# A GEGLU by seven products on one core: the weight sums' first pair on VectorE, and two copies behind the second snapshot pair

## The chip, the cores and the metric

The kernel runs on one core of a Trainium2 chip. The time is that of the device in microseconds (us), from one launch on inputs that are already in its memory. The core has five engines that work side by side, each through a queue of its own: TensorE (PE in the profile, its weight loads PEld), VectorE (DVE), ScalarE (ACT), GpSimd (POOL) and SyncE (SP), which here issues the DMAs.

## What is computed

```python
B, S, Dm, Df = 1, 2048, 1024, 3584
def reference(x, w_gate, w_up, w_down):
    g = jnp.einsum("bsd,df->bsf", x, w_gate)
    u = jnp.einsum("bsd,df->bsf", x, w_up)
    h = _gelu(g) * u
    return jnp.einsum("bsf,fd->bsd", h, w_down)
```

`_gelu` is the tanh approximation. All inputs and the output are bfloat16.

## The kernel before

**Seven products in place of eight.** Each matrix product is cut into 2 x 2 blocks and formed with seven block products (the Strassen-Winograd scheme) instead of eight. The price is sums of blocks: of the activations (`t1` to `t4`, made once a pass), of the weights (`s1` to `s4`, made for every unit), and of the results, which are gathered in PSUM and in float32 copies. Blocks that enter a sum are kept as fp32r; blocks that enter a product alone are cast (`sa` from the weights, `tb` from the activations).

**Stages.** There are two passes of 1024 rows of x (`NPASS`). In each, the gate and up products come first, in 14 units, and then the down product (`down`). A unit is 256 of the 3584 hidden columns, in two blocks of 128, for both gate and up (`GU`), by 1024 rows in two blocks of 512. The result is gelu(gate) x up in `hT`. In the first pass the first 8 units (`R = 8`, called the early units here; units are counted from 0) are opened ahead of time: `opening()` forms their first results from raw bfloat16 weights, and keeps of each the product P1 in float32 copies (`p1s`). When a unit's turn comes, P1 is copied back into two PSUM banks, `seed(u + 1, ...)` (line 540), so that further products can be added to it.

**A unit** is written out in `unit` (line 221). TensorE runs five pairs of products, one for gate and one for up, of four 128x512 matmuls each: P2 (`s2`, `t2`) into the seeded banks `e`; P5 (`s1`, `t1`) into other banks; P3 (`s3`, `t3`) into `e`; then one with `s4` and `tb` into the banks of P5; and P4 (`sa`, `t4`) into `e`. In the profile P2, P5 and P3 are the groups `bank<-t,s`, the fourth is `bank<-tb,s` and P4 is `bank<-t,sa`. In between:

- ScalarE copies the two `e` banks after P2 (the snapshots u2, line 108) and the two banks of P5 (the snapshots p5, line 108). In the early units these land in a part of `xT`, so the profile shows them as `xT<-bank`.
- After u2, `behind_u2` seeds the next unit (two ScalarE copies, line 540).
- VectorE adds p5 to `e` (`sum`, and the same for up into a PSUM bank), later u2 to the other banks, and multiplies gelu by up (`hT`).
- `prepare` (called as `after_p5`) makes the next unit's weight sums: `s1`, `s2`, `s3`, `s4`, two each, all on GpSimd (line 94), and the two casts `sa` on ScalarE (line 103).

The products add into banks that others read: P3 waits for the u2 snapshots, the `tb` product for the p5 snapshots, P4 for VectorE's two sums.

**Down-weight sums.** From unit 2 of the first pass on, each unit also makes the sums of one block of the down weights (`keep_part`, line 278). They have three parts. For each, ScalarE copies a raw bfloat16 half into a free PSUM bank (`bank<-raw`, line 278) and VectorE subtracts (`m`, line 91). Part 0 stands ahead of the u2 snapshots, parts 1 and 2 behind the seeds, ahead of the p5 snapshots; part 2 also needs part 1's result. SyncE then stores the three sums to device memory (`store_made`, line 289, 768 KB) and, behind this in the same queue, loads the next unit's two raw halves (`fetch_wd`, line 270, 256 KB each), and behind that, in some units, gate and up weights (line 127).

**Order.** SyncE, VectorE, GpSimd and TensorE follow the order of the program text throughout (`ORDER`), and ScalarE does so in the gate and up stage. The kernel has no planner there: what is written first is issued first on its engine, and an instruction that waits holds up all behind it on that engine.

Of the kernel before, what the change touches and what calls it, by code (L numbers as in the profile page):

```python
# [10 lines left out]
def kernel(  # L11
# [48 lines left out]
    R = 8  # L60
# [22 lines left out]
    def slot(shape, dtype, name):  # L83
        return kpool.tile(shape, dtype, name=name, tag="k")
# [5 lines left out]
    def dve(out, a, b, op):  # L90
        nc.vector.tensor_tensor(out=out, in0=a, in1=b, op=op)  # L91
# [4 lines left out]
    def new(eng, a, b, op, name, shape=None, dtype=None):  # L96
        t = slot(shape or [P, N], dtype or f32r, name)
        eng(t, a, b, op)
        return t

    def cast(src, name, shape=None):
        t = slot(shape or [P, N], f32r, name)
        nc.scalar.copy(out=t, in_=src)  # L103
        return t

    def snap(ps, name, at=None):
        t = slot([P, N], f32, name) if at is None else at
        nc.scalar.copy(out=t, in_=ps)  # L108
        return t
# [25 lines left out]
    def block_of(w, n):  # L135
        return [w[:, i, :, n * P : (n + 1) * P] for i in range(2)]

    def block(ip, u, h):
        return u + R * h if ip == 0 and u < R else 2 * u + h
# [8 lines left out]
    def sums_t(xT):  # L148
        K = range(KH)
        lo, hi = [[xT[c][:, k] for k in K] for c in range(2)], [  # L150
            [xT[c][:, KH + k] for k in K] for c in range(2)
        ]
        return Sums(
            how={
                "t1": lambda q: [new(dve, lo[1][k], lo[0][k], SUB, "t1") for k in K],
                "t2": lambda q: [new(dve, hi[1][k], q["t1"][k], SUB, "t2") for k in K],
                "t3": lambda q, K=K: [new(dve, hi[1][k], lo[1][k], SUB, "t3") for k in K],
                "t4": lambda q: [new(dve, hi[0][k], q["t2"][k], SUB, "t4") for k in K],
                "tb": lambda q: [cast(hi[1][k], "tb") for k in K],
            }  # L160
        )

    def sums_s(w, eng):
        GU = range(2)
        sh = [P, KH, P]
        a11, a21 = [[w[h][i][:, :KH] for i in GU] for h in range(2)]
        a12, a22 = [[w[h][i][:, KH:] for i in GU] for h in range(2)]
        return Sums(
            how={
                "s1": lambda q, GU=GU: [new(eng, a21[i], a22[i], ADD, "s1", sh) for i in GU],  # L170
                "s2": lambda q: [new(eng, q["s1"][i], a11[i], SUB, "s2", sh) for i in GU],
                "s3": lambda q: [new(eng, a11[i], a21[i], SUB, "s3", sh) for i in GU],
                "s4": lambda q: [new(eng, a12[i], q["s2"][i], SUB, "s4", sh) for i in GU],
                "sa": lambda q: [cast(a22[i], "sa", sh) for i in GU],
            }
        )
# [6 lines left out]
        t.make("t1", "t2", "t3", "tb", "t4")  # L183
        return t

    def make_s(w, eng):
        s = sums_s(w, eng)
        s.make("s1", "s2", "s3", "sa", "s4")
        return s

    def gelu(src):
        g = slot([P, N], f32, "g")
        nc.scalar.activation(g, src, ACT.Gelu_apprx_tanh)  # L193
        return g

    def times(fb, c, g, u):
        dve(hT[:, fb // NJ, fb % NJ, c, :], g, u, MUL)

    def product(ps, lhs, rhs, start):
        for k in range(KH):  # L200
            matmul(ps, lhs[:, k, :], rhs[k], start and k == 0, k == KH - 1)
# [10 lines left out]
    def add(ps, other):  # L212
        g = new(dve, ps[0], other[0], ADD, "sum", dtype=f32)
        dve(ps[1], ps[1], other[1], ADD)
        return g, ps[1]
# [5 lines left out]
    def unit(fbs, banks, s, t, spare, behind_u2, after_p5, aside, keep, ahead_of_p4, behind_p4):  # L221
        GU = range(2)
        e, c, d = banks
        for i in GU:
            product(e[i], s["s2"][i], t["t2"], False)
        aside()
        keep(0, c[0])
        u2 = [snap(e[i], "u2", spare[i]) for i in GU]
        behind_u2()
        keep(1, c[0])  # L230
        keep(2, c[1])
        up = c[1]
        c = d
        for i in GU:
            product(c[i], s["s1"][i], t["t1"], True)
        p5 = [snap(c[i], "p5", spare[2 + i]) for i in GU]
        after_p5()
        for i in GU:
            product(e[i], s["s3"][i], t["t3"], False)
        g = new(dve, e[0], p5[0], ADD, "sum", dtype=f32)  # L240
        dve(up, e[1], p5[1], ADD)
        for i in GU:
            product(c[i], s["s4"][i], t["tb"], False)
        times(fbs[1], 1, gelu(g), up)
        g, up = add(c, u2)
        times(fbs[0], 1, gelu(g), up)
        ahead_of_p4()
        for i in GU:
            product(e[i], s["sa"][i], t["t4"], False)
        behind_p4()  # L250
        times(fbs[1], 0, gelu(e[0]), e[1])
# [108 lines left out]
    sa = {}  # L360
# [142 lines left out]
    first = [block_of(wa, u) for u in range(2)] + [block_of(mid, u) for u in range(4)]  # L503
    first += [block_of(end, u) for u in range(2)]

    def early(u):
        if u // 2 not in pairs_of:
            pairs_of[u // 2] = load_w((R + u) // 2, new_w())
        return [first[u], block_of(pairs_of[u // 2], u % 2)]
# [3 lines left out]
    s, t = sums_s(early(0), dve), sums_t(xT)  # L513
# [24 lines left out]
    def seed(u, e):  # L538
        for i in range(2):
            nc.scalar.copy(out=e[i], in_=p1s[u][i])  # L540
# [70 lines left out]
    def weights(ip, u):  # L611
        return early(u) if ip == 0 and u < R else loaded(u)

    for ip in range(NPASS):
        with tc.manual_schedule(engines={ENG.Activation}):
            if ip == 0:
                ws = {}
                nxt = opening()
            else:
                raw_of(0, F)()  # L620
                raw_of(1, C)()
            for u in range(NU):
                js = making(u) if ip == 0 else []

                def behind_u2():
                    if ip == 0 and u + 1 < R:
                        seed(u + 1, F if u % 2 else C)

                def prepare():
                    if "s" not in nxt and u + 1 < NU:  # L630
                        nxt["s"] = make_s(weights(ip, u + 1), pool)
                    if len(js) == 1:
                        store_made(js[0])
                    for j in js[1:]:
                        keep_whole(j)
                    if ip == 0:
                        fetch_wd(making(u + 1))

                def keep(part, ps):
                    if js:  # L640
                        keep_part(js[0], part, ps)

                def aside():
                    if u + 2 < NU:
                        weights(ip, u + 2)

                def ahead_of_p4():
                    if u % 2 and u + 1 < NU and (ip or u + 1 >= R):
                        raw_of(u + 1, F)()
                        nxt["c11"] = raw_of(u + 2, C)  # L650

                def behind_p4():
                    if "c11" in nxt:
                        nxt.pop("c11")()

                if u % 2 and (ip or u):
                    E, K, C = C, E, K
                banks = (E, K, C) if u % 2 else (F, K, E)
                unit(
                    [block(ip, u, h) for h in range(2)], banks, s, t,  # L660
                    [None] * 4 if ip else spare0,
                    behind_u2, prepare, aside, keep, ahead_of_p4, behind_p4,
                )
                s = nxt.pop("s", None)

        last = ip == NPASS - 1
        got, nxt = {}, {}

        def more(step):
            if last:  # L670
                return
            if step in (-1, 0, 2):
                store_made({-1: NJ - 3, 0: NJ - 2, 2: NJ - 1}[step])
            if step == 0:
                xT[:] = new_x()
            if step >= 24 and step % 2 == 0 and step // 2 - 12 < len(moves):
                c, ko = moves[step // 2 - 12]
                transposing(xT, c, ko, (2 * (ip + 1) + c) * N)
            if step == 50:
                ws.clear()  # L680
                loaded(0), loaded(1)
            if step == 58:
                got["s"] = make_s(loaded(0), dve)
            if step == 62:
                got["t"] = make_t(xT)

        down(ip, F + K, C + E, last, more)
        E, K, C, F = K, E, F, C
        if not last:
            t, s = got["t"], got["s"]  # L690
# [29 lines left out]
```

## Time and profile before

| what | value |
|---|---|
| three runs | 543.8, 541.96, 542.95 us; median 542.95 |
| the profiled execution | 542.84 us, of which the span from first to last instruction is 541.0 us |
| granted TensorE clock | 1.00 in every stage |
| GpSimd | 246.3 us busy, 46% of the span |
| early units 0 to 6 | about 35 to 102 us |
| idle TensorE that waits for p5 snapshots (`xT L108`) | 2.3 us, 4 times |
| idle weight loads that are put down to GpSimd's `s` | 2.4 us, 3 times |
| ScalarE's down-weight copies waiting for raw rows, 53 to 108 us | 6.3 us, 5 times |

A line of the order of time has the start in us, the length in us, the engine, the line of the kernel, the operation, result and operands with buffer numbers left out, and the count; in brackets the idle time of the engine just before it and what ended that. Two instructions in a merged line overlap a little at their ends, so the step from one to the next is shorter than the length of one. A line of the stretches has from and to in us, the length, the busy time of TensorE and the number of its matmuls, its granted clock, the share of the DMA engines and GB/s. Some matmuls are missing from the record.

### The profile page before, as it was taken

How to read it: one execution, taken by the hardware profiler on the slowest of the kernel's cores; microseconds unless marked ns; L12 is line 12 of the kernel's file. 1: busy time of each engine (PE TensorE's matmuls, PEld its weight loads, DVE VectorE, ACT ScalarE, POOL GpSimd, SP SyncE). 2: the span in 40 equal slices, each digit the busy share in tenths (PEclk: the TensorE clock that was granted, in tenths of full speed). 3: DMA queues.
4: the chain of work that ended last, by engine and by line, in shares of the span. 5: the costliest groups of instructions: out<-in, count | busy, mean ns of one | idle time of the engine just before them, and what ended most of it. 6: DMA issues, size and time to landing. Idle time of an engine off the chain costs nothing.

```text
span 541.0 us, 7444 instructions
## 1 busy us (share of the span) xinstructions
PE 534.3 (99%) x2399; PEld 383.6 (71%) x2399; DVE 335.4 (62%) x517; ACT 272.3 (50%) x487; POOL 246.3 (46%) x221
## 2 busy tenths in 40 slices
PE   9999999999999999999999999999999999999997
PEld 5468877767677746888868676776868685488885
DVE  1686576667676895594965464555554639676730
ACT  4676776866666410165345555555555551114431
POOL 0049999996772500000086767676766600000000
PEclk9999999999999999999999999999999999999999
DMA  8954275857491999979863222242520049473751
GB/s 242 258 121 119 98 224 161 237 177 233 118 267 56 363 380 300 312 180 265 290 174 99 78 79 78 79 117 53 142 63 18 0 154 389 177 233 98 229 191 49
DMA packets 106471, 93.29 MB, mean 172 GB/s; under 512 B 17088, under 2 KB 91840, under 8 KB 106432
## 3 DMA queue, kind: packets, MB, share of 16 engines
q1 hardware_dynamic: 106432, 92.82, 58.5%
q8 instruction: 19, 0.31, 0.3%
q14 instruction: 20, 0.16, 0.1%
HBM read 74.45 MB, written 15.20 MB: 166 GB/s over the span
## 4 chain that ended last, share of the span: by engine, by line
PE 94%; ACT 3%; DMA 1%; DVE 1%; issue 1%; SPq 0%; ACTq 0%; DVEq 0%
PE bank L115 93%; DMA raw<-in_w_down_dram 1%; ACT xT L108 1%; ACT bank L540 1%; ACT bank L278 1%; PE bank L544 1%; PE bank L461 0%; DVE t L91 0%; ACT tb L103 0%; DVE m L91 0%; DVE hT L91 0%; ACT g L193 0%; ACT st L419 0%; DVE xT L467 0%; SPq L289 0%
## 5 line engine op out<-in xcount | busy, mean ns | idle before, releaser
L94 POOL TENSOR_TENSOR s<-w 128x512 fp32r<-128x512 bf16 x92 | 106.9, 1184 | 136.7 <-DVE t L91 86.0
L115 PE MATMUL bank<-t,s 128*128 128x512 f32 x672 | 157.6, 390 | 0.1
L115 PEld LDWEIGHTS bank<-t,s 128*128 128x128 f32 x672 | 126.1, 188 | 26.8 <-POOL s L94 0.4
L91 DVE TENSOR_TENSOR hT<-g,bank 128x512 bf16<-128x512 f32 x112 | 76.4, 687 | 18.5 <-ACT g L193 7.5
L193 ACT ACTIVATE g<-sum 128x512 f32<-128x512 f32 x76 | 48.3, 635 | 69.0 <-DVE sum L91 67.0
L115 PE MATMUL bank<-xT,w 128*128 128x512 bf16 (+1 forms) x360 | 78.7, 375 | 0.2 <-DVE xT L467 0.2
L108 ACT COPY p<-bank 128x512 f32<-128x512 f32 x92 | 52.6, 589 | 44.5 <-PE bank L115 43.6
L91 DVE TENSOR_TENSOR sum<-bank,p 128x512 f32<-128x512 f32 x34 | 23.5, 692 | 75.3 <-PE bank L115 71.1
L115 PEld LDWEIGHTS <-w 128*128 128x128 bf16 x360 | 34.0, 98 | 41.4 <-issue 2.6
L115 PE MATMUL bank<-q 128*128 128x512 f32 x240 | 59.0, 389 | 0.0
L115 PEld LDWEIGHTS <-hT 128*128 128x128 bf16 x320 | 31.1, 98 | 38.0 <-issue 0.9
L115 PE MATMUL bank<-tb,s 128*128 128x512 f32 x224 | 55.7, 391 | 2.3 <-ACT xT L108 2.3
L115 PE MATMUL bank<-t,sa 128*128 128x512 f32 x224 | 57.3, 398 | 0.0
L115 PEld LDWEIGHTS bank<-q 128*128 128x128 f32 x240 | 45.1, 188 | 9.3
L115 PEld LDWEIGHTS bank<-tb,s 128*128 128x128 f32 x224 | 41.7, 188 | 12.5 <-POOL s L94 2.0
L115 PEld LDWEIGHTS bank<-t,sa 128*128 128x128 f32 x224 | 42.1, 188 | 9.5
L115 PE MATMUL bank<-raw,hT 128*128 128x512 bf16 x224 | 48.7, 379 | 0.0
L103 ACT CAST tb<-raw 128x512 fp32r<-128x512 bf16 x28 | 17.3, 626 | 62.2 <-DMA raw<-in_w_down_dram 26.6
L94 POOL TENSOR_TENSOR s<-w,s 128x512 fp32r<-128x512 bf16 x40 | 46.1, 1175 | 0.0
L94 POOL TENSOR_TENSOR s<-s,w 128x512 fp32r<-128x512 f32 x40 | 45.8, 1167 | 0.0
L91 DVE TENSOR_TENSOR q<-hT 128x512 fp32r<-128x512 bf16 x56 | 38.4, 686 | 4.3 <-PE bank L115 4.3
L108 ACT COPY xT<-bank 128x512 f32<-128x512 f32 x56 | 30.8, 592 | 6.4 <-PE bank L115 6.2
(54 smaller groups left out, 569.2 us busy)
## 6 DMA issues: line engine op xcount, KB each, us to landing
raw<-in_w_down_dram SPq DMA_DIRECT2D x76, 256.0 KB, 4.8
q<-td SPq DMA_DIRECT2D x60, 256.0 KB, 4.9
w<-in_w_gate_dram SPq DMA_DIRECT2D x24, 512.0 KB, 4.9
w<-in_w_up_dram SPq DMA_DIRECT2D x24, 512.0 KB, 6.2
td<-m SPq DMA_DIRECT2D x12, 768.0 KB, 4.5
w<-td SPq DMA_DIRECT2D x6, 1024.0 KB, 9.8
out_dram<-st SPq DMA_DIRECT2D x32, 128.0 KB, 1.7
hT<-in_w_gate_dram SPq DMA_DIRECT2D x3, 512.0 KB, 4.9
```

The costliest lines, as they stand in the source:

```text
L91: nc.vector.tensor_tensor(out=out, in0=a, in1=b, op=op)
L94: nc.gpsimd.tensor_tensor(out=out, in0=a, in1=b, op=op)
L103: nc.scalar.copy(out=t, in_=src)
L108: nc.scalar.copy(out=t, in_=ps)
L115: nc.tensor.matmul(ps, lhsT=lhs, rhs=rhs, start=start, stop=stop, skip_group_check=True)
L193: nc.scalar.activation(g, src, ACT.Gelu_apprx_tanh)
L278: nc.scalar.copy(out=ps, in_=a)
L540: nc.scalar.copy(out=e[i], in_=p1s[u][i])
L544: nc.tensor.matmul(bank[3], lhsT=warm[:, :P], rhs=warm, start=True, stop=True)
```

## The change

Two edits. In units 1 to 6 of the first pass, `prepare` has the next unit's `s1` pair made by VectorE instead of GpSimd (units 2 to 7 get theirs so). And in the units that seed a next one (0 to 6; down-weight sums exist from unit 2), parts 1 and 2 of the down-weight sums are called behind the p5 snapshots instead of ahead of them; they use the same banks by their names from before the swap (`banks[1]`).

```diff
-    def make_s(w, eng):
+    def make_s(w, eng, first=None):
         s = sums_s(w, eng)
-        s.make("s1", "s2", "s3", "sa", "s4")
+        if first:
+            s["s1"] = sums_s(w, first)["how"]["s1"](s)
+            s.make("s2", "s3", "sa", "s4")
+        else:
+            s.make("s1", "s2", "s3", "sa", "s4")
         return s
...
         u2 = [snap(e[i], "u2", spare[i]) for i in GU]
-        behind_u2()
-        keep(1, c[0])
-        keep(2, c[1])
+        seeded = behind_u2()
+
+        def keep_on():
+            keep(1, banks[1][0])
+            keep(2, banks[1][1])
+
+        if not seeded:
+            keep_on()
         up = c[1]
         c = d
         for i in GU:
             product(c[i], s["s1"][i], t["t1"], True)
         p5 = [snap(c[i], "p5", spare[2 + i]) for i in GU]
+        if seeded:
+            keep_on()
         after_p5()
...
                 def behind_u2():
                     if ip == 0 and u + 1 < R:
                         seed(u + 1, F if u % 2 else C)
+                        return True
 
                 def prepare():
                     if "s" not in nxt and u + 1 < NU:
-                        nxt["s"] = make_s(weights(ip, u + 1), pool)
+                        by = dve if ip == 0 and u + 1 < R else None
+                        nxt["s"] = make_s(weights(ip, u + 1), pool, by)
```

On VectorE the two `s1` sums of a unit now stand behind parts 1 and 2 of the down-weight sums and ahead of `sum`; on ScalarE the two p5 snapshots stand ahead of the two copies of parts 1 and 2, and these ahead of the `sa` casts. The orders of TensorE and SyncE are as before.

## The prediction

> **What bounds the kernel now.** I read the page's busy line first, then the stretches of the early units, then the order of time inside one unit.
>
> ```profile
> PE 534.3 (99%) x2399; PEld 383.6 (71%) x2399; DVE 335.4 (62%) x517; ACT 272.3 (50%) x487; POOL 246.3 (46%) x221
> ```
>
> TensorE is idle for 541.0 - 534.3 = 6.7 us only, so the change can win little and can lose any time by which it makes TensorE wait. The chain of waits is TensorE alone from 98.53 us to 537.70 us: nothing behind the early units absorbs a delay made in them. Next the stretches that begin with the first product of units 0 to 6 (the first number is the length):
>
> ```profile
> 34.84:44.15 9.31, 9.31 (x43) 1.00 0.09 16
> 44.15:53.22 9.07, 9.07 (x42) 1.00 0.58 160
> 53.22:62.30 9.08, 9.08 (x41) 1.00 0.29 87
> 62.30:71.81 9.51, 9.35 (x42) 1.00 0.44 135
> 71.81:81.68 9.87, 9.31 (x41) 1.00 0.84 240
> 81.68:92.28 10.60, 9.59 (x41) 1.00 0.39 123
> 92.28:102.28 10.00, 9.35 (x41) 1.00 0.84 236
> ```
>
> An undisturbed unit of 40 matmuls is 9.07 us (unit 1), so eight matmuls are 1.81 us. Units 2 to 6 take 102.28 - 53.22 = 49.06 us against 5 x 9.07 = 45.35: they lose 3.71 us. That is all a repair of these units can bring. Who is late shows in the order of time in unit 4:
>
> ```profile
> 71.81 5.60 PE L115 MATMUL bank<-t,s 128*128 128x512 f32 x24
> ...
> 73.67 0.59 ACT L278 CAST bank<-raw 128x512 f32<-128x512 bf16 x1 [1.23 <-DMA raw<-in_w_down_dram]
> 74.20 1.07 ACT L108 COPY xT<-bank 128x512 f32<-128x512 f32 x2
> ...
> 76.19 1.12 ACT L278 CAST bank<-raw 128x512 f32<-128x512 bf16 x2
> 76.83 1.49 DVE L91 TENSOR_TENSOR m<-bank,m 128x512 fp32r<-128x512 f32 x2 [1.84 <-ACT bank L278]
> 77.23 1.08 ACT L108 COPY xT<-bank 128x512 f32<-128x512 f32 x2
> ...
> 77.97 2.06 PE L115 MATMUL bank<-tb,s 128*128 128x512 f32 x8 [0.56 <-ACT xT L108]
> ...
> 78.23 0.68 DVE L91 TENSOR_TENSOR sum<-bank,xT 128x512 f32<-128x512 f32 x1
> 78.34 0.34 SPq L289 DMA_DIRECT2D td<-m  x1
> 78.79 1.32 SPq L270 DMA_DIRECT2D raw<-in_w_down_dram  x2
> ...
> 79.87 1.98 PE L115 MATMUL bank<-t,sa 128*128 128x512 f32 x8
> ...
> 84.27 0.59 ACT L278 CAST bank<-raw 128x512 f32<-128x512 bf16 x1 [1.85 <-DMA raw<-in_w_down_dram]
> ```
>
> ScalarE's queue stands until the raw down-weights land (73.67); the u2 snapshots, the seeds (75.15 and 75.67), two more down-weight copies (76.19) and the p5 snapshots (77.23) follow without a gap, and the tb products wait 0.56 us for the first p5. The raw rows themselves come late because they stand behind the store of the down-weight sums on SyncE's queue, and this waits for VectorE's last m. So there is **a loop from unit to unit**: first copy, u2, seeds, copies, m, store, load, first copy. From first copy to store it is 4.67 us each time (63.76 to 68.43, 73.67 to 78.34, 84.27 to 88.94, 94.23 to 98.90); from store to the next first copy 4.83, 5.24, 5.93, 5.29 and 5.26 us (stores at 58.93, 68.43, 78.34, 88.94, 98.90; copies at 63.76, 73.67, 84.27, 94.23, 104.16). A turn, 9.9 to 10.6 us, is longer than 9.07: this loop, not TensorE, paces units 3 to 6.
>
> **The change, part by part.** (a) The p5 snapshots pass ahead of two copies of 0.52 us (issue to issue: 74.20, 75.15 are two copies, 75.15, 75.67 one). p5 comes 1.04 us earlier, and the waits of the tb products (0.16, 0.56, 0.96 and 0.65 us, together 2.33) go. P5 itself ends 3.6 us after the unit's start, before ScalarE reaches its snapshots, so these add no wait of their own.
>
> (b) The price of (a) is on the other two queues. The two copies, and the two m that need them, start 1.04 us later behind the first copy; so first copy to store becomes 4.67 + 1.04 = 5.71 us. SyncE's queue holds the next raw loads behind that store, and they hold the next unit's first copy. Units 2 to 6 each add 1.04 to the loop: 5 x 1.04 = 5.20 us by unit 7, whose first copy moves from 104.16 to 109.36.
>
> (c) VectorE gets two s1 sums in six units (those made in units 1 to 6). The opening has this row: two of them from the same kind of operands took 1.29 us at 31.86, the next instruction started 1.20 later; so 0.60 each. They stand in VectorE's order behind both m and ahead of `sum`. Queued behind them are `sum` and the second PSUM sum, which read the banks into which P4 (t,sa) accumulates: P4 waits for `sum`. Before, `sum` starts 0.11 us ahead of the store (78.23, 78.34); now it starts 1.20 - 0.11 = 1.09 behind it. In unit 2 the store moves to 58.93 + 1.04 = 59.97, `sum` to 61.06, and P4 can start 0.69 + 0.15 later (0.15 is what lies between the end of a first p5 copy, 77.23 + 0.59, and 77.97): 61.90, where TensorE would be there at 53.22 + 7.25 = 60.47. That is **a new wait of 1.4 us on TensorE**, longer than any wait removed. In unit 1 there are no m; the s1 issue near 45.5 (behind the last hT, 44.83) and `sum` is due at 48.95: hidden by 2.2 us, and the same 1.2 us are lost if that cover goes.
>
> (d) GpSimd loses 12 of its sums (1.17 us each, rows of 2.25 a pair). It was nearly full (8 x 1.13 = 9.0 of 9.07 us), but now it waits for s1: in unit 2 s1 are ready at about 61.1, s2 at 62.3 and 63.4, the next unit's P2 asks for them at 61.90 + 1.81 = 63.7 and 64.6. Hidden by 1.4 and 1.2 us, and only because P4 waits; I count neither gain nor loss.
>
> (e) The down-weight copies use the banks by their old names and no bank is written earlier than before. The s1 wait for weights: the last load that matters here was issued at 70.76 and is used in unit 5, after 90 us; nothing.
>
> **The sum.** By (b) the store of unit 6 moves from 98.90 to 104.10; `sum` follows 1.09 later, 105.19; P4 at 106.03; P4 is 1.81: unit 7 starts at 107.84 instead of 102.28, +5.56. One small addition: in the turn with the shortest landing (4.83) the first copy is held by ScalarE's own order instead: from `sum`, 0.78 to its gelu, 0.68 to hT, 0.60 each to the next two sums, then two gelu and a copy, some 3.9, so 1.09 + 3.9 = 5.0 behind the store; +0.1. Unit 7 has no seeds and keeps its old order: first copy 109.4, first p5 0.52 + 1.04 + 1.04 later, TensorE can go on 0.7 behind that at 112.7, and gets there at 107.84 + 5.44 = 113.3: no wait, no loss, nothing regained. So +5.6 us in total: span 541.0 to 546.6; this execution took 542.84 (1.8 around the span), which would be 548.4, and the median of 542.95 becomes **548.5 us**. Apart, the order of the copies alone gives store 104.10, `sum` 103.99, unit 7 at 106.64, +4.4; VectorE's s1 the other 1.2, once, since the loop doesn't pass through them.
>
> **Unknown costs.** The landing of raw behind the store: rows from 4.83 to 5.93. All turns at the floor of 5.0 instead of 5.24, 5.93, 5.29: -1.5, so +4.1. All four at 5.93 instead of 4.83, 5.24, 5.29: +1.1 + 0.7 + 0.6 = +2.4, so +8.0. I take the rows as they are, since order and sizes on the queue are the same. VectorE's second s1 beside GpSimd's first s2: before has no VectorE sum of two SBUF operands beside a busy GpSimd in these units; from nothing (GpSimd starts only when the first s1 is written, by when the second is issued) to one GpSimd sum, 1.18 us; I take nothing. The Trainium skill, "SBUF — State Buffer", section "Who interferes with whom", speaks against the change: a VectorE instruction with two SBUF inputs and a GpSimd one that reads SBUF exclude one another, and the second to issue waits for the whole of the first. Were it always VectorE that came second, `sum` would be later by up to that one GpSimd row in each unit; by the order above GpSimd comes second, and has room. No row here shows the case.
>
> **Rivals.**
> - *The raw rows don't follow the store* (they land late for another reason, DMA load, say). For it: the landing varies by 1.1 us with no change in the queue. Against: all five intervals are 4.8 to 5.9. Then only the P4 wait counts: 9.07 + 1.4 = 10.47 a unit, 52.35 for five, +3.3 by 49.06: 546.2 us. Chance 0.08.
> - *Faster:* p5 is early and `sum` is in time all the same, so TensorE loses nothing in units 2 to 6: -3.7, 539.2 us. It decides from the point where `sum` starts no later than 7.25 - 0.84 = 6.4 us behind the unit's start; I work out 7.8 in unit 2 (61.06 - 53.22). For it: VectorE has some 3 us free in a unit. Against: the free time lies ahead of the m, and its order is fixed. Chance 0.05.
> - *Worse:* slow landings throughout, or s1 held behind GpSimd sums so that ScalarE's gelu, too, hold the first copy (5.0 + 1.2 = 6.2 a turn in place of 5.3, four turns, +3.6, and 1.2 at the end): 551 to 553 us. Chance 0.09.
> - *The change does nothing here:* the waits only swap names, 543 us. Against: s1 and the copies do stand elsewhere in the queues. Chance 0.02.
>
> **How the numbers follow.** The forecast (548.5) has 0.76; its own bounds are +4.1 and +8.0, 547.0 to 551.0. The first rival's 546.2 is taken in, the low end by some of the 0.9 us by which a run can miss the median: 546.0 to 551.0. Faster than 542.95 by more than 0.3% (1.6 us, about what a measurement of this kernel can tell from none) 0.05, the same 0.02, slower 0.93.
>
> **What would show it.** Right: units 2 to 6 of 10.4 to 11.7 us; no tb wait for p5; an idle TensorE ahead of t,sa of 1.4 to 2.5 us with VectorE's `sum` as the releaser; first copy to store 5.7; GpSimd idle before each s2 until VectorE's s; everything behind unit 7 moved as one. Wrong: `sum` ahead of P3's end, first copies no later in their unit than before, or a store that doesn't slip.

## The result, and the profile after

The changed kernel takes 547.21 us in the median of 6 runs (546.97 to 548.1), beside 543.32 us for the kernel before (6 runs, 541.96 to 544.64): a ratio of 1.0074, 95% interval 1.0058 to 1.0091. It is slower by 3.9 us. The profiled execution took 546.97 us, with a span of 545.2 us against 541.0.

The page's busy line:

```profile
PE 533.2 (98%) x2380; PEld 383.5 (70%) x2399; DVE 342.9 (63%) x529; ACT 273.0 (50%) x487; POOL 235.1 (43%) x209
```

VectorE has 12 instructions more and GpSimd 12 fewer. TensorE was idle for 6.7 us and is now idle for 545.2 - 533.2 = 12.0; a part of this is only missing from the record, which has 2380 matmuls in place of 2399. The stretches from the first product of each of units 1 to 6 to that of the next (from, to, length, TensorE's busy time and matmuls, its clock, DMA share, GB/s):

```profile
44.02:53.08 9.06, 9.06 (x41) 1.00 0.55 153
53.08:63.55 10.47, 9.36 (x41) 1.00 0.28 85
63.55:74.14 10.59, 9.38 (x42) 1.00 0.39 116
74.14:85.00 10.86, 9.38 (x41) 1.00 0.76 227
85.00:95.51 10.51, 9.38 (x41) 1.00 0.39 118
95.51:106.46 10.95, 9.38 (x41) 1.00 0.76 215
```

Unit 1 is as before. Units 2 to 6 take 106.46 - 53.08 = 53.38 us where they took 49.06. From the start of unit 7 to the end it is 545.2 - 106.46 = 438.7 us, and before 541.0 - 102.28 = 438.7: all of the loss lies in five units, and nothing is regained behind them.

Inside unit 4 of the changed kernel, in order of time:

```profile
74.14 5.61 PE L115 MATMUL bank<-t,s 128*128 128x512 f32 x24
...
75.57 0.59 ACT L289 CAST bank<-raw 128x512 f32<-128x512 bf16 x1 [0.29 <-DMA raw<-in_w_down_dram]
...
78.10 1.08 ACT L108 COPY xT<-bank 128x512 f32<-128x512 f32 x2
79.06 1.13 ACT L289 CAST bank<-raw 128x512 f32<-128x512 bf16 x2
...
79.59 1.98 PE L115 MATMUL bank<-tb,s 128*128 128x512 f32 x8
79.70 1.49 DVE L91 TENSOR_TENSOR m<-bank,m 128x512 fp32r<-128x512 f32 x2 [2.81 <-ACT bank L289]
...
81.11 1.28 DVE L91 TENSOR_TENSOR s<-w 128x512 fp32r<-128x512 bf16 x2
81.22 0.34 SPq L300 DMA_DIRECT2D td<-m  x1
...
82.31 0.68 DVE L91 TENSOR_TENSOR sum<-bank,xT 128x512 f32<-128x512 f32 x1
...
83.05 2.12 PE L115 MATMUL bank<-t,sa 128*128 128x512 f32 x8 [1.48 <-DVE sum L91]
...
86.09 0.59 ACT L289 CAST bank<-raw 128x512 f32<-128x512 bf16 x1
```

The p5 snapshots (78.10) are in time and the `tb` products (79.59) no longer wait: the edit does what it says. But the two copies start at 79.06, the two m behind them at 79.70, the two s1 at 81.11 and `sum` only at 82.31, and P4 stands 1.48 us for it. The bracket of the m shows that VectorE had nothing to do for 2.81 us just ahead of them. The last line has no bracket: this first copy found its raw rows there and waited only for ScalarE's own queue, unlike the one at 75.57. From 53 to 112 us, units 2 to 6 and most of unit 7, the waits read:

```profile
PEld bank L115 <- DVE sum L91: 8.6, 5, 2.0
PE bank L115 <- DVE sum L91: 6.5, 5, 1.6
...
ACT bank L289 <- DMA raw<-in_w_down_dram: 0.9, 3, 0.4
```

The first number is the us in total, then the times and the longest. TensorE waits 6.5 us for `sum`, where before it waited 2.3 us for the p5 snapshots; ScalarE's wait for raw rows shrank from 6.3 to 0.9 us.

The chain of work that ended last, followed back from the end, says the same. Before, one landing of raw rows lies on it (78.79 to 84.25); in the changed kernel none does. From P4 of unit 2 to P4 of unit 3 it reads (start, length, engine, result and line; the m stand between the down-weight copy and the s1):

```profile
61.60 3.94 PE bank L115 x16
...
65.57 0.73 ACT xT L108 x2
66.30 1.01 ACT bank L551 x2
...
67.70 0.61 ACT xT L108
68.31 0.50 ACT bank L289
...
70.84 0.69 DVE s L91
71.52 0.61 DVE sum L91
...
72.18 3.96 PE bank L115 x16
```

P4 and the next unit's P2, then u2, seeds, p5, a down-weight copy, the m, the s1, `sum`, and P4 again: **a second loop from unit to unit**, 72.18 - 61.60 = 10.58 us round, which passes through the s1 and not through the store. From unit 4 to 5 and from 5 to 6 the chain goes from `sum` through gelu and `hT` to the next u2 instead.

### The profile page after: what moved, and what is told of

It reads as the page before. It is cut to its first block, busy times and chain, and to the rows that moved or that the text cites. A ratio compares the mean times of both kernels' runs of the same rounds, so it can differ in the third digit from the quotient of the medians.

```text
span 545.2 us, 7416 instructions
## 1 busy us (share of the span) xinstructions
PE 533.2 (98%) x2380; PEld 383.5 (70%) x2399; DVE 342.9 (63%) x529; ACT 273.0 (50%) x487; POOL 235.1 (43%) x209
## 4 chain that ended last, share of the span: by engine, by line
PE 90%; ACT 4%; DVE 4%; issue 2%; ACTq 0%; DVEq 0%
PE bank L115 89%; ACT xT L108 2%; DVE m L91 1%; DVE sum L91 1%; DVE hT L91 1%; ACT bank L551 1%; DVE s L91 1%; ACT g L197 1%; PE bank L555 1%; PE bank L472 0%; ACT bank L289 0%; DVE t L91 0%; ACT tb L103 0%; ACT st L430 0%; DVE xT L478 0%
## 5 line engine op out<-in xcount | busy, mean ns | idle before, releaser
L94 POOL TENSOR_TENSOR s<-w 128x512 fp32r<-128x512 bf16 x80 | 93.1, 1185 | 130.2 <-DVE t L91 86.0
L115 PE MATMUL bank<-xT,w 128*128 128x512 bf16 (+1 forms) x349 | 76.3, 374 | 0.9 <-DVE xT L478 0.2
```

The source lines that it names most:

```text
L94: nc.gpsimd.tensor_tensor(out=out, in0=a, in1=b, op=op)
L115: nc.tensor.matmul(ps, lhsT=lhs, rhs=rhs, start=start, stop=stop, skip_group_check=True)
```

## The experiments

In the table, "units 2 to 6" is from the first product of unit 2 to that of unit 7 in the profiled execution. It is the cleaner measure: unit 0 starts up to 0.94 us apart in these executions (34.69 to 35.63), behind stages that no edit touches.

| kernel | units 2 to 6, us | median, us | before beside it, us | ratio, 95% interval |
|---|---|---|---|---|
| before | 49.06 | 543.32 | | |
| changed | 53.38 | 547.21 | 543.32 | 1.0074 (1.0058 to 1.0091) |
| order of the copies alone | 51.95 | 546.34 | 542.96 | 1.0066 (1.0051 to 1.0081) |
| s1 on VectorE alone | 48.45 | 542.27 | 542.96 | 0.9991 (0.9982 to 1.0001) |
| before, raw rows early | 45.47 | 539.43 | 542.96 | 0.9933 (0.9916 to 0.9950) |
| changed, raw rows early | 52.54 | 546.25 | 542.96 | 1.0064 (1.0049 to 1.0079) |
| changed, s1 ahead of the m | 51.96 | 546.59 | 542.43 | 1.0075 (1.0060 to 1.0090) |
| changed, both | 46.52 | 540.53 | 542.43 | 0.9967 (0.9956 to 0.9977) |
| before, raw rows early, s1 ahead of the m | 45.51 | 539.56 | 542.43 | 0.9944 (0.9929 to 0.9959) |
| before, profiled again | 48.71 | 542.6, one run | 542.43 | |

**The order of the copies alone.** GpSimd makes all sums again.

```diff
-                        by = dve if ip == 0 and u + 1 < R else None
+                        by = None
```

> The order of the copies alone; GpSimd makes s1 as before. Theory (the raw rows behind the store pace the early units, and the copies lengthen that loop by about 1 us a unit): first copy to store 5.6 us instead of 4.67, TensorE waits for VectorE's sum in units 3 to 6 by about 1 us or more, +3 to +4.4 us, 546 to 547.5 us. Rival (only the two s1 on VectorE cost anything): the p5 waits of 2.3 us go and nothing comes in their place, 541 to 543 us.

Measured 546.34 us, +3.4. The waits in units 2 to 6 of this kernel:

```profile
ACT bank L289 <- DMA raw<-in_w_down_dram: 5.1, 4, 1.5
PE bank L115 <- DVE sum L91: 3.7, 4, 0.9
```

With no s1 on VectorE, TensorE still waits for `sum` in units 3 to 6, because everything in the unit starts from a first copy that waits up to 1.5 us for raw rows. From first copy to store it is 5.65 us (64.61 to 70.26) where it was 4.67. In this kernel the chain that ended last holds three landings of raw rows (from 60.24, 81.60 and 102.92). The copies cost most of the loss, and through the store's loop; the rival falls.

**s1 on VectorE alone.** The seeding units call the copies where they stood.

```diff
                         seed(u + 1, F if u % 2 else C)
-                        return True
```

> s1 on VectorE alone; the copies stand ahead of p5 as before. Theory: the loop from first copy to first copy does not pass through s1, so the later sum costs once, in unit 6: +0.4 to +0.6 us, 543 to 544.2 us, with the P4 wait taking the place of the p5 waits inside each unit. Rival (s1 ahead of sum costs in every unit): five times up to 1.2 us less what the p5 waits give back, +2.5 to +6 us, 545.5 us or more.

Measured 542.27 us, and the interval touches 1: no measurable cost, against +2.5 us or more by the rival. That it is 0.4 to 0.6 us slower, as the theory had it, isn't shown either. In the profile units 2 to 6 are 0.61 us shorter than before. One interval accounts for this: from the store of unit 4 to the next first copy the kernel before has 5.93 us, this one 4.88 (78.27 to 83.15). If those 1.05 us have another cause, the s1 cost 1.05 - 0.61 = 0.44 here, an estimate. The last experiment looks at that interval.

**Raw rows early, in the kernel before.** The two raw halves for units 3 to 7 are asked for one unit sooner, ahead of the store instead of behind it.

```diff
                 def aside():
+                    if ip == 0 and 2 <= u < R - 1:
+                        fetch_wd(making(u + 1))
                     if u + 2 < NU:
...
-                    if ip == 0:
+                    if ip == 0 and not 2 <= u < R - 1:
                         fetch_wd(making(u + 1))
```

> The kernel before, with the raw rows of units 4 to 7's sums (and those of unit 3) asked for one unit earlier, ahead of the store. Theory (the raw rows pace units 3 to 6): first copies wait no more, units 2 to 6 come down to 9.1 us, -3 to -3.7 us, 539.3 to 540 us. Rival (GpSimd, 9.0 us of sums in a unit, or ScalarE's queue paces them): units stay at 9.5 us or more, 542 to 543.5 us.

Measured 539.43 us, -3.5. The stretches of its units 2 to 6:

```profile
53.91:63.00 9.09, 9.09 (x41) 1.00 0.30 90
63.00:72.09 9.09, 9.09 (x42) 1.00 0.45 140
72.09:81.17 9.08, 9.08 (x41) 1.00 0.91 276
81.17:90.27 9.10, 9.10 (x42) 1.00 0.43 131
90.27:99.38 9.11, 9.11 (x41) 1.00 0.91 254
```

Length and busy time of TensorE are equal in each: it never waits. So the kernel before lost its 3.6 us here to late raw rows alone. Neither ScalarE's queue with the p5 snapshots in their old place nor GpSimd's 9.0 us of sums paces it, and these two are what the change set out to relieve.

**Raw rows early, in the changed kernel.** The same edit.

> The changed kernel with the same early loads. Theory: the first copies then wait only for ScalarE's own order (gelu behind VectorE's late sum); the 0.29, 0.38 and 0.25 us that three of them still waited go, -0.5 to -1 us, units 2 to 6 of 10.5 us each, 546.2 to 546.8 us: the loop through VectorE's sum is as long as the one through the store. Rival (the store's loop alone paces the changed kernel): units down to 10 us or less, -2.5 us or more, below 545 us.

Measured 546.25 us; units 2 to 6 are 0.84 us shorter, 10.47 to 10.57 each, and no first copy waits for raw rows. TensorE waits for `sum` as before (1.10 to 1.20 us in each unit, 5.7 in all). What freed the kernel before is worth little here: the second loop is as long.

**s1 ahead of the two m, in the changed kernel.** The two sums are written behind the seeds, so that on VectorE they stand between the m of part 0 and that of part 1, in the time in which it waited for ScalarE.

```diff
                         seed(u + 1, F if u % 2 else C)
+                        if u:
+                            nxt["s1"] = sums_s(early(u + 1), dve)["how"]["s1"](None)
                         return True
...
-                        nxt["s"] = make_s(weights(ip, u + 1), pool, by)
+                        nxt["s"] = make_s(weights(ip, u + 1), pool, nxt.pop("s1", None))
```

> The changed kernel with the two s1 sums of VectorE moved ahead of the two m of parts 1 and 2, into the time in which VectorE waits for ScalarE; sum is then 1.2 us earlier in its unit. Theory (two chains of nearly equal length: through the store and the raw rows, and through sum and gelu; taking one alone away leaves the other): as with the order of the copies alone, 546 to 546.8 us, 0.5 to 1 us below the changed kernel, first copies waiting 1 to 1.5 us for raw rows again. Rival (s1 ahead of sum is what costs): back to 543 us.

Units 2 to 6 take 51.96 us, as with the copies' order alone (51.95) and 1.42 less than the changed kernel. The first copies wait for raw rows again, by 0.97 to 1.50 us. In the median it is no gain (1.0075 beside 1.0074): in the profiled execution unit 2 starts 0.88 us later than in the changed kernel's, by what lies ahead of unit 0, and I can't say whether that belongs to the kernel. The rival, 543 us, falls.

**Both.** Raw rows early and s1 ahead of the m, in the changed kernel.

> The changed kernel with both: raw rows asked for a unit earlier, and s1 ahead of the m. Each alone is worth 1 us at most by the theory. Theory: both chains are gone, units 2 to 6 come down from 10.7 to about 9.5 us, with some 0.3 to 0.5 us of wait for sum left that the late copies cause; 540.5 to 542 us, 5 to 6.5 us below the changed kernel. Rival (the two gains add): 545.5 us.

Measured 540.53 us. Units 2 to 6 drop by 53.38 - 46.52 = 6.86 us, where the two edits alone brought 0.84 and 1.42, together 2.26. That is the sign of two loops side by side: each alone leaves the other in place. Put the other way, each alone makes nearly the whole loss: s1 ahead of `sum`, with the raw rows early, costs 52.54 - 46.52 = 6.02 us, 1.2 a unit; the raw rows behind the store, with s1 ahead of the m, cost 51.96 - 46.52 = 5.44. The next kernel differs from this one only in the place of the copies and takes 45.51 us: the 1.01 between them are the price of the late copies. In the waits of this kernel's units 2 to 6 the weight loads of P4 stand for `sum` five times, by 0.4 us at most:

```profile
PEld bank L115 <- DVE sum L91: 1.8, 5, 0.4
```

**The version that is faster than both.** The kernel before with raw rows early, and s1 on VectorE ahead of the m.

> The kernel before with raw rows asked for a unit earlier, the copies in their old place, and s1 on VectorE ahead of the m. Theory: with the raw rows early the units already take 9.1 us on TensorE alone, so GpSimd's relief brings nothing: 539 to 540 us, as with the early raw rows alone. Rival (GpSimd's 9.0 us in a unit still cost something): 538 us or less.

Measured 539.56 us, and 539.43 without s1 on VectorE: units of 9.09 to 9.11 us in both. Once the raw rows are early, GpSimd's relief brings nothing. They are 2.9 and 3.5 us faster than the kernel before beside them, and the changed kernel's median lies 7.7 to 7.8 us above theirs. What s1 ahead of `sum` costs with raw rows early and the copies in their old place was not run.

**The kernel before, profiled again.**

> The kernel before, profiled again, for the interval of 5.93 us from the store of unit 4 to the next first copy, which the changed kernel and the one with s1 alone do not show (4.87 and 4.88). If it belongs to this kernel (an instruction load of 16 KB falls into this transfer in its profile): 5.8 to 6 us again, with an instruction packet in 78 to 85 us. If it was chance: 4.8 to 4.9 us, and a span some 1 us shorter.

The interval is there again: the store at 78.49, the next first copy at 84.15, 5.66 us, where the other three turns that end in a first copy of unit 4, 6 or 7 have 5.23 to 5.26 and the one of unit 3, the only other without weights behind the raw rows, has 4.82. The DMA queues of this execution in 78 to 85 us (packets, MB, share of the 16 engines):

```profile
q1 hardware_dynamic: 432, 1.31, 57.7%
q8 instruction: 1, 0.02, 1.0%
...
td<-m SPq DMA_DIRECT2D x1, 768.0 KB, 5.0
raw<-in_w_down_dram SPq DMA_DIRECT2D x2, 256.0 KB, 5.3
```

And of the kernel with s1 alone, in the same stretch, in which its store is at 78.27:

```profile
q14 instruction: 1, 0.01, 0.3%
...
td<-m SPq DMA_DIRECT2D x1, 768.0 KB, 4.1
raw<-in_w_down_dram SPq DMA_DIRECT2D x2, 256.0 KB, 4.6
```

The transfers are the same; in the kernel before one packet of 16 KB on the instruction queue falls among them, and they land 0.7 to 0.9 us later. In the changed kernel, too, only a q14 packet falls between the store (81.22) and the next first copy, and the interval is 4.87.

All six profiles with the raw rows behind the store have such a packet of 16 KB on q8, between 74.8 and 79.5 us, and what is in flight then lands late in each. With the order of the copies alone it falls on the second raw half, 6.4 us from issue to landing where the turn of unit 5 has at most 5.0; with s1 ahead of the m likewise, 6.3. The first copy needs the first half only and is in its usual place (5.24 and 5.22 behind the store). In the changed kernel and with s1 alone it falls on gate and up weights: 7.4 and 8.4, 7.1 and 8.1 us, where the turn of unit 5 has 5.9 or 6.0 and 7.1. So it depends on when the packet comes whether a first copy is late. The cause is inferred from these coincidences; no run moved the packet alone.

## Why the prediction was right, and where its sizes were off

The forecast was 548.5 us, from 546.0 to 551.0, slower by 5.6; it is slower by 3.9, from 543.32 to 547.21. Step by step:

- **What bounds the early units** (the loop through store and raw load): shown for the kernel before, which loses nothing in units 2 to 6 with the raw rows early. In the changed kernel this loop is one of two, and the chain that ended last goes by the other.
- **(a) the tb waits go:** yes; there is no wait for p5 left in units 2 to 6.
- **(b) 1.04 us longer from first copy to store:** it is 0.97 or 0.98 (64.71 to 70.35, 75.57 to 81.22, 86.09 to 91.73, 97.04 to 102.68 are 5.64 or 5.65, forecast 5.71), since what now stands ahead of the copies is two snapshots, 0.96 us (78.10 to 79.06), and not two copies of 1.04. The prediction had that step in its own lines, 74.20 to 75.15.
- **(c) s1 cost 0.60 each ahead of `sum`, and P4 waits:** 1.20 from the first s1 to `sum` (81.11 to 82.31); `sum` 1.09 behind the store, as forecast. In unit 2 it starts at 60.87 (61.06 forecast) and the unit takes 10.47 us, which is the 9.07 + 1.4 worked out. The wait itself was forecast at 1.4 to 2.5 us; it is 1.11 to 1.57, and only in two units of five above 1.4, since about 0.3 us of each unit's loss stand in its busy time (9.36 to 9.38 us, 9.06 in unit 1). The hidden place in unit 1 held: 9.06 us, no wait. On top of the copies' order the s1 add 53.38 - 51.95 = 1.43 in five units (1.2 forecast, once), 1.17 of it in unit 2 (10.47 against 9.30). But the reason given, that the loop doesn't pass through them, holds for the store's loop alone: the second one does, and with the raw rows early they cost 1.2 in every unit of the changed kernel.
- **(d) GpSimd waits for s1 and nobody for GpSimd:** its s2 begin at 81.93 in unit 4 after 3.73 us of idling, and TensorE has no wait for `s` of GpSimd in these units.
- **The +0.1 from ScalarE's own order** was the right mechanism, taken too lightly: in two turns of five (first copies at 64.71 and 86.09) that chain, not the raw rows, released the first copy, 4.93 and 4.87 us behind the store. The experiments show both chains to be of nearly one length.

The start of unit 7 was forecast 5.56 us later (102.28 to 107.84) and is 4.18 later (106.46). **The step that was mis-sized is the landing behind the store:** I took the rows "as they are, since order and sizes on the queue are the same", and carried the 5.93 us of one turn over. Measured there: 4.87, so -1.06. The rest: unit 2 starts 0.14 sooner, the five turns slip by 0.97 or 0.98 (0.99 in unit 2) instead of 1.04, together -0.32, and the other landings and the last step add 0.14. The sum is -1.06 - 0.14 - 0.32 + 0.14 = -1.38, which is the difference of 5.56 and 4.18. That row stood apart from the other four, 4.83 to 5.29, and came, as far as the coincidences tell, of a packet that in the changed kernel falls on other transfers; the low end of the range covered it. The same landing is in the +4.4 forecast for the order of the copies alone, which measured +3.4.

The rival that the raw rows don't follow the store (+3.3, 546.2) lies near the measured time, but its cause is refuted: asking for the rows ahead of the store took 3.5 us off the kernel before. Its price was right for the second loop: with the raw rows early the changed kernel takes 52.54 us for the five units, and the rival had 52.35. So it is partly luck that the forecast, added up along the store's loop, came as near as it did: the other loop alone gives +3.3 by the rival, and +3.9 was measured. The faster rival needed `sum` within 6.4 us of the unit's start; it came 7.8 us behind in unit 2 (60.87 - 53.08) and 8.2 in unit 4 (82.31 - 74.14).

## What to carry to other kernels

When an engine waits inside a stage that repeats, look for a chain that runs from one turn into the next, queue by queue, and compare its length with the busy time of the bounding engine: here the visible wait was for a snapshot, and the cause was a load queued behind a store. Moving work behind the visible wait then lengthens the chain by what now stands ahead of that work, here 0.97 us a turn. Look for a second loop of the same length before repairing one: here each repair alone brought 0.84 and 1.42 us, and both 6.86. And where an engine has free time, ask where in its order that time lies: the same two sums cost 1.4 us over five units where they stand ahead of `sum` (6.0 with the raw rows early), and nothing ahead of the m.

## What the runs showed of the hardware

- A transfer that met one packet of 16 KB on the q8 instruction queue landed about 0.7 to 1.5 us later, in six profiles of six: the store and raw halves in both profiles of before, the second raw half or the gate and up weights in the others. In two turns with a q14 packet (0.01 MB) the store landed as in turns without (4.1 us). That the packet is the cause is inferred from this coincidence in time.
- In the turns where 1 MB of gate and up weights is queued behind the raw rows, these land later, too: in the kernel with the copies' order alone 5.22 to 5.26 us from store to first copy, against 4.81 us in the turns without.
- VectorE's s1 and GpSimd's sums hold one another up where they meet. All operands lie in SBUF. In 44 to 48 us of the changed kernel (ns: least, median, most):

```profile
L91 DVE TENSOR_TENSOR s<-w x2: 679/822/966, 45.3 to 46.2; 128x512 fp32r<-128x512 bf16 x2
L94 POOL TENSOR_TENSOR s<-s,hT x2: 1172/1330/1487, 46.4 to 47.9; 128x512 fp32r<-128x512 f32 x2
```

  The first s1 started at 45.30 beside a GpSimd sum that ran to 45.72 and took 966 ns instead of 679; the first s2 started at 46.41 beside the second s1 and took 1487 instead of 1172. The Trainium skill, "SBUF — State Buffer", section "Who interferes with whom", says that two such instructions contend, and that the contention is an exclusive lock; here the second to start was longer by some 0.3 us in both cases, less than the 0.42 and 0.46 us that the first had left to run by this profile, whose spans of GpSimd are rough. In units 2 to 6 the first s2 is longer in the same way (1475 to 1487 ns) and the s1 are not (681 to 685): there VectorE lost nothing, as the prediction took it.
